# The second half of five loads on a second queue, and one cast on another engine

## The chip, the cores and the metric

The kernel runs on one core of a Trainium2 chip. The metric is the device time of one execution in microseconds (us), the median of several executions. The profile is that of one execution. Engines are named as the profile does: PE (TensorE), DVE (VectorE), ACT (ScalarE), POOL (GpSimd), SP (SyncE, which here only issues DMAs). A letter q behind an engine means its instruction queue: it issues or waits while the engine itself is idle.

## What is computed

A local and a pooled attention for 8 batches of 8 heads (576 positions, 64 elements), whose sum goes through a layer that mixes positions and channels:

```
q_d, k_d, v_d = means of 4 neighbouring positions of q, k, v        # 144 positions
out_up        = softmax(q_d k_d^T / 8) v_d, each position repeated 4 times
out_local     = softmax(q k^T / 8 where |i - j| < 4) v
x             = (out_up + out_local), heads side by side            # 8 x 576 x 512
theta         = x w_theta
u             = x + w_tok_r (x cos theta) + w_tok_i (x sin theta)
out           = u + max(u w_ch, 0)
```

Inputs and output are float32; the kernel works in bfloat16 with float32 sums.

## The kernel before

The kernel is a set of small generators, one for each step (load, cast, turns, scores and so on), each of which goes through all batches. A string, ORDER (line 66), says by one letter after the other which generator takes its next step; every instruction is pinned behind the one before it on its own engine (`pin`, line 758). So ORDER sets the order of the work on each engine, and nothing moves at run time: an engine whose next instruction waits lets nothing behind it pass. That holds for DMA issues too, which stand in the program order of the engine that issues them. ENGINES (line 86) names by one letter the engine of each copy or cast: v for VectorE, a for ScalarE, p for GpSimd.

**Loads** (`load`, line 220, letter L). A batch has 13 items in the order k0 k1 q0 q1 k2 k3 q2 q3 v0 v1 v2 v3 v4. A k or q item is one DMA of 128 partitions and 288 KB. A v item is two DMAs of 64 partitions and 128 KB each, one for each half of the partitions, since the two windows of positions that it holds overlap (line 225). Each item lands in one of 15 staging tiles, used in turn, and all loads are issued by SP. So batch 0 and the first two items of batch 1 find free tiles; a later item waits until the cast that read its tile is done.

The DMAs of the two hardware queues, SP's and ScalarE's, take eight completion semaphores in turn, and a DMA is issued when the earlier one with its semaphore has landed. Before, all are on SP: the first v DMA waits for k0, the next for k1, then q0, q1, k2 and so on.

**Casts** (`cast`, line 233, letter C) turn an item into bfloat16. In batch 0 the engines are: k0 and k1 VectorE; q0, q1 and k2 GpSimd; k3 ScalarE; q2 and q3 GpSimd; v0, v2, v4 ScalarE; v1, v3 GpSimd. The instruction is recorded at line 124.

**What follows for batch 0.** `turns` (line 291) transposes k and q on TensorE, 9 blocks for each of four pairs of items: k0 with k1, q0 with q1, k2 with k3, q2 with q3 (line 297). `turns_out` (line 300) copies the four results out of PSUM as kT and qT, for batch 0 all on ScalarE, where they stand right behind the cast of k3. `query_sums` (line 320; for batch 0 on VectorE, line 326) and `key_sums` (line 309, VectorE, line 314) add four neighbouring positions. `scores` and `scores_exp` (lines 465, 477) make the local scores and their exponentials, `masks` (line 485, VectorE) cuts them to the band. `pooled_scores` and `pooled_exp` (lines 379, 391, 398) do the pooled ones, `pooled_out` (lines 411, 417) multiplies with the pooled v, and `pooled_norm` divides on VectorE, beginning with the reciprocal at line 430. `outputs` (line 497) multiplies the masked scores with v.

On VectorE the order in this stretch is: constants, the sum of queries (326), two sums of keys (314), the second sum of queries, the first mask (485), and then the cast of batch 1's k0. On ScalarE it is: the table of functions, the cast of k3, four copies of kT and qT, the cast of v0, an exponential, the cast of v2, a pooled exponential (398), the cast of v4, and the next exponential (477).

The later steps (phases, mix, channels, lines 575 to 743) are large matmuls of 128 x 512 and make up most of TensorE's time.

Of the kernel before, what the change touches and what calls it, by code (L numbers as in the profile page):

```python
# [26 lines left out]
W = 64  # L27
# [18 lines left out]
def kernel(  # L46
# [11 lines left out]
    nc = tc.nc  # L58
# [5 lines left out]


    ORDER = (
        "kkLkLLCkkkLCLCCALCACALkCaLCAaakkkaeLSLLkkLCLsdCLSCCdeLmPLpLLCLCOLLoOCLLUluusPSpsALxCoiCxNLmCinnNaLnl"
        "nAllCClCdlLLAALLamaCaQeeTOOqdCooilitSLTtLLOPsLpoPTpmTliSCtHTCCUllstthuOHuoXmhXHlyOliyoOxxhVCHoiNhiCA"
        "CNlnvGnnCXnyCalAgOVQoVaTiqvVSvTCvtAstaCmCZVAHVVaOvovSVTLvsLTivetStXTlXytHVsHGlmVvHVvVhzLyLvhVvLLVgXe"
        "hVVLvvVvVJdjLyLLLLhJJCvCvLOvljOSJLmjoloCdsCCiCJilJjUOLjuuPPLpZCoClxziJmjxjpACXNaNyLLAnnCCCnOLXJanLyA"  # L70
# [14 lines left out]
    )  # L85
    ENGINES = dict(
        C=(
            "vvpppappapapavppvaaapvppppppppppppappppppapapappapvappappppppaapaaavvpapppapaapavvaapappaaapapaa"
            "vpaavpaa"
        ),  # L90
        a="aaaaaaaaaavaaaaavaaaaaaaaaaaaava",
# [2 lines left out]
        v="avaavaavvvvavvvava",  # L94
# [119 lines left out]
    def stage(key):  # L214
        t = staged[key] = rot("st", [P, S], FP32, 15)
        return t
# [3 lines left out]
    def load(b):  # L220
        for it in ITEMS:
            c = int(it[1])
            if it[0] == "v":
                t = stage((b, it))[:, 0:DM].rearrange("p (h d) -> p h d", d=D)
                for g in range(2):
                    lo = W0[2 * c + g]
                    nc.sync.dma_start(out=t[W * g:W * g + W], in_=v[b, :, lo:lo + W, :].rearrange("h p d -> p h d"))  # L227
            else:
                src = k if it[0] == "k" else q
                nc.sync.dma_start(out=stage((b, it)), in_=src[b, 2 * c:2 * c + 2].rearrange("h (p r) d -> (h p) (r d)", r=WR))  # L230
            yield
# [536 lines left out]
    def each(steps, n=B):  # L768
# [3 lines left out]
    sequences = {  # L772
        "k": constants(), "1": table(AF.Sin), "2": table(AF.Exp),
        "L": each(load), "C": each(cast), "l": weight_loads(), "V": weight_turns(), "v": weight_turns_out(),
        "A": each(turns), "a": each(turns_out), "d": each(key_sums), "e": each(query_sums),
        "U": each(pooled_v), "u": each(pooled_v_out), "x": each(pooled_v_last),
# [49 lines left out]
```

## Time and profile before

| what | us |
| --- | --- |
| three runs | 235.08, 233.96, 234.40 |
| their median | 234.4 |
| the profiled execution, its own time | 234.87 |
| its span, first to last instruction | 233.0 |
| busy: PE, DVE, ACT, POOL | 210.3, 196.1, 149.9, 83.1 |

The clock granted to TensorE was 0.991 of full speed on average. The hardware queue that SP feeds had packets in the 16 DMA engines for 82.2% of their span. Times in the profile count from the first instruction. A row of the timeline has the start, the length, the engine, the line, the operation, what it writes and reads, and in brackets how long the engine stood idle before it and what ended that. A line of the chain has a start, a length and what filled it.

### The profile page before, as it was taken

The page shows a single profiled execution, that of the slowest core. Times are in us where ns is not written, and L with a number is a line of the kernel's source. Part 1 is how long each engine was busy: PE and PEld are TensorE (multiplying, and loading weights), DVE is VectorE, ACT ScalarE, POOL GpSimd, SP SyncE. Part 2 cuts the span into 40 slices and gives each one's busy share as a digit, 9 for nine tenths or more (in the row PEclk, how much of TensorE's full clock was granted, in tenths as well). Part 3 has the DMA queues.
Part 4 walks back from the last instruction along what each step waited for, and adds up shares of the span by engine and source line. Part 5 has one row for each costly group of instructions (what it writes and reads, how often), then busy time and mean ns, then how long its engine had stood idle before and what let it go on. Part 6 is the DMA issues. An engine that isn't in the chain of part 4 may idle for free.

```text
span 233.0 us, 8062 instructions
## 1 busy us (share of the span) xinstructions
PE 210.3 (90%) x3309; PEld 134.1 (58%) x3344; DVE 196.1 (84%) x402; ACT 149.9 (64%) x220; POOL 83.1 (36%) x125
## 2 busy tenths in 40 slices
PE   0547959999999999999999999999999999999993
PEld 0435845877787547656666647565655674446441
DVE  3797998998988999998999888977999988395463
ACT  2376968999687976877899988399156366500000
POOL 1434987992555575534621503404032000000000
PEclk9999997999999999999999999999999999999999
DMA  6989999989997997996999999999135693858566
GB/s 205 284 188 344 201 182 334 258 123 176 341 225 148 264 303 146 254 275 149 260 277 264 183 197 347 256 244 217 19 70 138 93 171 126 124 165 214 125 187 251
DMA packets 87061, 48.52 MB, mean 208 GB/s; under 512 B 71920, under 2 KB 74352, under 8 KB 87024
## 3 DMA queue, kind: packets, MB, share of 16 engines
q1 hardware_dynamic: 84016, 44.84, 82.2%
q0 software_dynamic: 2496, 2.38, 7.2%
q10 hardware_dynamic: 512, 0.79, 1.0%
q8 instruction: 26, 0.43, 0.8%
q14 instruction: 11, 0.09, 0.2%
HBM read 34.11 MB, written 9.44 MB: 187 GB/s over the span
## 4 chain that ended last, share of the span: by engine, by line
PE 78%; DMA 8%; DVE 7%; SPq 4%; issue 2%; ACT 0%; DVEq 0%; ACTq 0%
PE space L668 30%; PE space L711 12%; PE space L575 11%; PE space L297 4%; PE space L537 3%; DMA st<-in_v_dram 3%; SPq L227 3%; PE space L497 3%; DMA st<-in_q_dram 2%; PE space L465 2%; DMA st<-in_k_dram 2%; PE space L627 2%; DVE tmp L517 2%; PE space L717 1%; PE space L411 1%
## 5 line engine op out<-in xcount | busy, mean ns | idle before, releaser
L668 PE MATMUL space<-WT,z 128*128 128x64 bf16 (+2 forms) x562 | 74.3, 284 | 1.1 <-issue 0.5
L668 PEld LDWEIGHTS <-z 128*128 128x128 bf16 x576 | 38.2, 98 | 28.7 <-issue 0.4
L575 PE MATMUL space<-wth,xT 128*128 128x512 bf16 x116 | 31.3, 388 | 0.7 <-issue 0.2
L711 PE MATMUL space<-wch,uT 128*128 128x512 bf16 (+1 forms) x125 | 31.2, 373 | 0.4
L684 DVE TENSOR_TENSOR uT<-space,xT 128x512 bf16<-128x512 f32 (+2 forms) x36 | 22.1, 620 | 8.0 <-PE space L668 7.8
L517 DVE TENSOR_TENSOR tmp<-space,rl 128x512 bf16<-128x512 f32 x40 | 26.7, 681 | 0.8 <-DVE rl L511 0.2
L560 DVE TENSOR_TENSOR xT<-space,xdT 128x464 bf16<-128x464 f32 (+3 forms) x42 | 24.5, 605 | 3.1 <-PE space L537 3.0
L477 ACT ACTIVATE pm<-space 128x1024 bf16<-128x1024 f32 (+1 forms) x24 | 21.1, 882 | 9.2 <-PE space L465 7.4
L582 ACT ACTIVATE cs<-space,pihc 128x512 bf16<-128x512 f32 x32 | 22.4, 700 | 5.4 <-PE space L575 2.9
L331 POOL TENSOR_TENSOR two<-qT 128x576 f32<-128x576 bf16 x14 | 17.2, 1229 | 20.8 <-ACT qT L124 20.6
L314 DVE TENSOR_REDUCE kd<-kT 128x290 bf16<-128x1160 bf16 x16 | 21.5, 1349 | 0.0
L124 POOL CAST q_tm<-st 128x576 bf16<-128x576 f32 x20 | 13.5, 677 | 18.8 <-DMA st<-in_q_dram 18.8
L725 DVE SCALAR_TENSOR_TENSOR osb<-space,ur 128x512 f32<-128x512 f32 x28 | 19.1, 682 | 1.1 <-PE space L711 1.0
L297 PE MATMUL space<-ident,k_tm 128*128 128x128 bf16 x144 | 12.5, 242 | 7.6 <-DVE k_tm L124 7.1
L583 ACT ACTIVATE cs<-space 128x512 bf16<-128x512 f32 x32 | 19.4, 607 | 0.0
L711 PEld LDWEIGHTS <-uT 128*128 128x128 bf16 x132 | 12.1, 98 | 11.8
L124 ACT COPY qT<-space 128x1152 bf16<-128x1152 bf16 x16 | 18.0, 1127 | 1.3 <-PE space L297 0.9
L124 POOL CAST v_w<-st 128x512 bf16<-128x512 f32 x19 | 12.6, 664 | 17.5 <-DMA st<-in_v_dram 13.4
L124 POOL CAST k_tm<-st 128x576 bf16<-128x576 f32 x16 | 11.2, 702 | 19.2 <-DMA st<-in_k_dram 19.0
L124 ACT COPY kT<-space 128x1152 bf16<-128x1152 bf16 x13 | 14.6, 1124 | 5.1 <-PE space L297 5.1
L575 PEld LDWEIGHTS <-xT 128*128 128x128 bf16 x128 | 11.5, 99 | 10.3 <-issue 0.5
L485 DVE TENSOR_TENSOR pm<-pm,band 128x1024 bf16<-128x1024 bf16 (+1 forms) x24 | 16.4, 693 | 1.0 <-ACT pm L477 1.0
(93 smaller groups left out, 369.7 us busy)
## 6 DMA issues: line engine op xcount, KB each, us to landing
st<-in_v_dram SPq DMA_DIRECT2D x80, 128.0 KB, 5.1
st<-in_k_dram SPq DMA_DIRECT2D x32, 288.0 KB, 5.3
st<-in_q_dram SPq DMA_DIRECT2D x32, 288.0 KB, 5.6
out_dram<-osb SPq DMA_DIRECT2D x28, 256.0 KB, 3.4
out_dram<-osb SPq DMA_DIRECT2D x6, 128.0 KB, 3.4
uT<-in_moe_w_tok_r_dram POOLq DMA_DIRECT2D x6, 108.0 KB, 6.6
uT<-in_moe_w_tok_i_dram POOLq DMA_DIRECT2D x6, 108.0 KB, 5.5
wth<-in_moe_w_theta_dram POOLq DMA_DIRECT2D x4, 128.0 KB, 6.5
```

The source lines that it names most:

```text
L124: copies[next(engines[step])](**operands)
L297: nc.tensor.transpose(out=ps[:, P * r:P * r + P], in_=(k_tm if what == "k" else q_tm)[:, i, r, :, :], identity=ident)
L314: nc.vector.tensor_reduce(out=kd[:, hs, :, 0:PG].rearrange("p e g m -> p (e g) m"), axis=AX.X, op=ALU.add, in_=kT[:, hs, :].rearrange("p e ...
L477: nc.scalar.activation(out=pm.rearrange("p e c j w -> p e (c j w)"), in_=held.pop(("S", b, u))[:, :, 0:4 * W * n], func=AF.Exp, scale=SCL)
L517: nc.vector.tensor_tensor(out=tmp.rearrange("p g (j d) -> p g j d", d=D), in0=held.pop(("loc", b, c))[:, :, :, 0:D], in1=rls.pop((b, c)).u ...
L560: nc.vector.tensor_tensor(out=xTs[b][i][:, :, lo:lo + n].rearrange("p e (m j) -> p e m j", j=4), in0=ps[:, :, at:at + n].rearrange("p e (m ...
L575: nc.tensor.matmul(out=th, lhsT=xT[:, dc, P * c:P * c + P], rhs=wth[:, dc, :], start=(dc == 0), stop=(dc == 3))
L582: nc.scalar.activation(out=cs[:, 0, :], in_=th, func=AF.Sin, bias=pihc, scale=1.0)
L583: nc.scalar.activation(out=cs[:, 1, :], in_=th, func=AF.Sin, bias=0.0, scale=1.0)
L668: nc.tensor.matmul(out=ps[:, n * i:n * i + n], lhsT=z[:, j, P * d:P * d + P], rhs=WT[:, j, lo:lo + n], start=(j == 0), stop=(j == 8))
L684: nc.vector.tensor_tensor(out=uT[:, dc, lo:lo + m], in0=ps[:, 0:m], in1=xT[:, dc, lo:lo + m], op=ALU.add)
L711: nc.tensor.matmul(out=ps, lhsT=uT[:, dc, P * c:P * c + P], rhs=wch[:, dc, cols], start=(dc == 0), stop=(dc == 3))
```

## The change

Three edits go together.

1. In batch 0, the second half of each v load (g = 1) is issued by ScalarE's queue instead of SP's.
2. The third cast, that of q0 of batch 0, goes from GpSimd to ScalarE.
3. In ORDER, the loads from k3 to v4 of batch 0 come right after the third cast. Only the letters L move; without them the old and the new string are the same. On SP, which does nothing else there, this changes no order. It sets where ScalarE's five issues stand: behind its cast of q0 and ahead of its cast of k3.

```
     ORDER = (
-        "kkLkLLCkkkLCLCCALCACALkCaLCAaakkkaeLSLLkkLCLsdCLSCCdeLmPLpLLCLCOLLoOCLLUluusPSpsALxCoiCxNLmCinnNaLnl"
+        "kkLkLLCkkkLCLCLLLLLLLLCACACAkCaCAaakkkaeSkkCsdCLSCCdeLmPLpLLCLCOLLoOCLLUluusPSpsALxCoiCxNLmCinnNaLnl"
...
     ENGINES = dict(
         C=(
-            "vvpppappapapavppvaaapvppppppppppppappppppapapappapvappappppppaapaaavvpapppapaapavvaapappaaapapaa"
+            "vvappappapapavppvaaapvppppppppppppappppppapapappapvappappppppaapaaavvpapppapaapavvaapappaaapapaa"
...
                 for g in range(2):
                     lo = W0[2 * c + g]
-                    nc.sync.dma_start(out=t[W * g:W * g + W], in_=v[b, :, lo:lo + W, :].rearrange("h p d -> p h d"))
+                    queue = nc.scalar if b == 0 and g else nc.sync
+                    queue.dma_start(out=t[W * g:W * g + W], in_=v[b, :, lo:lo + W, :].rearrange("h p d -> p h d"))
```

The program that is built from it has on ScalarE, in this order: the table of functions, the cast of q0, the five issues, the cast of k3, and then what stood behind it before. The eight semaphores are still taken in turn, so that the waits of the v issues become:

| half | issued by | waits for the landing of |
| --- | --- | --- |
| v0, second | ScalarE | k0 |
| v0, first | SP | k1 |
| v1, second | ScalarE | q0 |
| v1, first | SP | q1 |
| v2, second | ScalarE | k2 |
| v2, first | SP | k3 |
| v3, second | ScalarE | q2 |
| v3, first | SP | q3 |
| v4, second | ScalarE | v0, second half |
| v4, first | SP | v0, first half |

The next load on SP, k0 of batch 1, waits for the landing of v1's second half, and k1 of batch 1 for v1's first half. The order of the instructions on TensorE and VectorE is the same as before; GpSimd lacks its first cast.

## The prediction

> **What bounds the kernel now.** The page comes first: the span, and the engines' shares of the chain that ended last.
>
> ```profile
> span 233.0 us, 8062 instructions
> PE 78%; DMA 8%; DVE 7%; SPq 4%; issue 2%; ACT 0%; DVEq 0%; ACTq 0%
> ```
>
> TensorE has 78% of the chain, so a change in the first 20 us counts only by how much later or earlier the long busy stretch begins. The busy time by stretches says where that stretch starts (columns: length, then busy us and instructions of PE, PEld, DVE, ACT, POOL, granted clock, DMA share, GB/s).
>
> ```profile
> 12.00:16.00 4.00, 2.62 (x81) 2.06 (x81) 3.82 (x8) 3.44 (x5) 0.95 (x2) 1.00 0.78 174
> 20.00:34.00 14.00, 10.37 (x216) 8.62 (x212) 13.82 (x25) 10.45 (x14) 12.04 (x19) 1.00 1.22 235
> 34.00:57.00 23.00, 22.20 (x439) 15.62 (x441) 20.97 (x47) 21.50 (x35) 18.09 (x29) 0.93 1.02 222
> 57.00:230.00 173.00, 169.99 (x2513) 104.08 (x2541) 148.88 (x280) 108.15 (x163) 47.70 (x65) 1.00 0.89 202
> ```
>
> From 20 to 34 us VectorE is busy 13.82 of 14.00; from 34 us TensorE is busy 22.20 of 23.00, then 169.99 of 173.00. Nothing after 20 us has room to give back a late start, and an early start would be kept too. So the question is how VectorE's work moves between 9 and 25 us. I read that stretch engine by engine in the timeline (start, length, engine, line, operation; in brackets the idle time before it and what ended it). ScalarE:
>
> ```profile
> 9.40 0.67 ACT L124 CAST k_tm<-st 128x576 bf16<-128x576 f32 x1 [7.38 <-DMA st<-in_k_dram]
> 9.98 1.11 ACT L124 COPY kT<-space 128x1152 bf16<-128x1152 bf16 x1
> 10.99 1.12 ACT L124 COPY qT<-space 128x1152 bf16<-128x1152 bf16 x1
> 18.37 0.89 ACT L398 ACTIVATE pd<-space 128x864 bf16<-128x864 f32 x1 [1.51 <-PE space L379]
> 19.66 1.03 ACT L477 ACTIVATE pm<-space 128x1024 bf16<-128x1024 f32 x1
> ```
>
> VectorE:
>
> ```profile
> 12.14 1.35 DVE L326 TENSOR_REDUCE qdT<-qT 128x288 bf16<-128x1152 bf16 x1 [1.23 <-ACT qT L124]
> 17.85 0.68 DVE L485 TENSOR_TENSOR pm<-pm,band 128x1024 bf16<-128x1024 bf16 x1
> 20.11 0.75 DVE L124 CAST k_tm<-st 128x576 bf16<-128x576 f32 x1 [1.58 <-DMA st<-in_k_dram]
> 25.11 0.19 DVE L430 RECIPROCAL rd<-space 72x8 f32<-72x8 f32 x1
> ```
>
> TensorE:
>
> ```profile
> 17.98 0.34 PE L379 MATMUL space<-qdT,kd 64*64 64x144 bf16 x4 [2.02 <-DVE qdT L326]
> 20.74 0.33 PE L379 MATMUL space<-qdT,kd 64*64 64x144 bf16 x4 [0.63 <-ACT pm L477]
> 21.59 0.62 PE L465 MATMUL space<-qT,kT 64*64 64x64 bf16 x16 [0.16 <-DVE vd L124]
> 22.18 1.12 PE L297 MATMUL space<-ident,k_tm 128*128 128x128 bf16 x9
> 23.59 0.87 PE L417 MATMUL space<-vd,pd 128*72 128x260 bf16 x2
> ```
>
> The chain of this stretch: the cast of k3 on ScalarE at 9.40, two copies behind it in program order, then VectorE's sum at 12.14, which had stood idle 1.23 for the second copy. From there VectorE runs without a gap to the end of the mask, 17.85 + 0.68 = 18.53, and then waits 1.58 for the first k load of batch 1. So **ScalarE's cast of k3 is on the path**, and behind it lies 1.58 of slack that a late load makes.
>
> **The change part by part.** *The third cast* (q0) leaves GpSimd for ScalarE.
>
> ```profile
> 6.12 0.66 POOL L124 CAST q_tm<-st 128x576 bf16<-128x576 f32 x1 [4.81 <-DMA st<-in_q_dram]
> 8.50 0.67 POOL L124 CAST k_tm<-st 128x576 bf16<-128x576 f32 x1
> 10.49 0.67 POOL L124 CAST q_tm<-st 128x576 bf16<-128x576 f32 x1 [1.32 <-DMA st<-in_q_dram]
> 11.67 0.67 POOL L124 CAST q_tm<-st 128x576 bf16<-128x576 f32 x1 [0.50 <-DMA st<-in_q_dram]
> ```
>
> q0 lands at 6.12. ScalarE takes 0.67 for that shape (its 9.40 row) and idled 7.38 up to 9.40, so the cast runs from 6.12 to 6.79 at no cost; GpSimd loses 0.66 where it idled. If that idle time were gone it would cost 0.67.
>
> *The five issues on ScalarE* follow this cast in its program order, and k3's cast stands behind all five. Each load waits for the semaphore that an earlier load used: v0's second half for k0, v1's for q0, v2's for k2, v3's for q2, and **v4's for the landing of v0's second half**. That such a wait holds a queue can be seen on SP, in the chain in order of time, where the fourth issue of v starts as q1 lands; the last two rows are a v issue that nothing held and the issue of batch 1's k0.
>
> ```profile
> 2.12 5.62 DMA st<-in_q_dram
> 7.75 0.94 SPq L227
> 12.66 0.63 SPq L227
> 14.69 0.62 SPq L230
> ```
>
> With 0.63 + 0.04 an issue: the first two at 6.8 and 7.5; the third needs k2, cast at 8.50 and so landed by then, and ends about 9.2; the fourth needs q2, landed at 10.49, and ends at 11.1; the fifth needs v0's second half. Its landing time is unknown. The nearest rows are the issues of v before, all ten and then the first alone (it sits in the 4.78 row):
>
> ```profile
> L227 SPq DMA_DIRECT2D st<-in_v_dram x10: 632/720/2522, 4.8 to 14.0; - x10
> DMA to landing us min/median/max: 3.3/5.0/7.3
> 4.78 0.81 SPq L227 DMA_DIRECT2D st<-in_v_dram  x1
> DMA to landing us min/median/max: 7.3/7.3/7.3
> ```
>
> Issued at 6.8 it lands between 6.8 + 3.3 = 10.1 and 6.8 + 7.3 = 14.1. I take 12.0, where its other half landed before (4.78 + 7.3): both share the engines with the same k and q loads. The median, 5.0, gives 11.8, nearly the same. So the fifth issue ends at 12.0 + 0.65, and k3's cast starts at 12.65, **D = 3.25 late**. At the early end the fourth issue decides, k3 starts at 11.8, D = 2.4; at the late end 14.75, D = 5.35.
>
> The trace shows the 16 DMA engines at a share of 0.78 between 12 and 16 us and of 1.02 and more in the busy stretches: there is a little room while v loads go out one at a time, and no more. [...]
>
> *What D does.* Everything from the copy at 9.98 to the mask is in program order behind k3's cast. VectorE's sum starts at 12.14 + 3.25, the mask ends at 18.53 + 3.25 = 21.78. The cast of batch 1's k0 no longer waits and starts at about 21.75 instead of 20.11: 1.65 late on this branch. The other branch has no such slack: the products at 17.98 wait for VectorE's sums, the exponential at 18.37 for them, the one at 19.66 stands behind it, and the products at 20.74 waited for that one. They come at 24.0. Behind them TensorE runs nearly closed up to the end of L417, 23.59 + 0.87 = 24.46, less the 0.16 that L465 need not wait any more: 24.46 + 3.25 - 0.16 = 27.55. VectorE's reciprocal at 25.11 reads that result, so it comes 27.55 - 25.11 = 2.4 late, the later of the two branches. From there VectorE was full.
>
> *The five issues taken from SP.* Nothing but loads stands behind them. Before, batch 1's k0 was issued at 14.69; now it waits for v1's second half, issued at 7.5, by the median landing at 12.5: about 2 earlier. That is worth at most VectorE's 1.58, already counted as slack here. GpSimd's queue carries no load of this stretch. v0 to v4 are cast behind the copies and are there in time.
>
> **Sum:** +3.25 (k3's cast) - 0.16 - 0.65 (24.46 to 25.11) = **+2.4 us**. The profiled execution took 234.87 (span 233.0), which gives 237.3; the median of the runs shown is 234.4, which gives **236.8**. With D = 2.4 the net is 1.6 (236.0), with D = 5.35 it is 4.5 (238.9).
>
> **Rivals.** *It is not slower.* The mechanism: ScalarE is free again when k3 lands, k0 of batch 1 lands earlier, and VectorE's wait of 1.58 goes with no other in its place. The gain ends at the other branch, whose result at 24.46 - 0.16 lies 0.8 ahead of 25.11: 234.4 - 0.8 = 233.6, and 232.7 if the cold stretch below goes too. For it speak the wait itself and the DMA share of 0.78. It decides if k3's cast starts less than 0.8 after 9.40; against it, the fourth issue waits for q2, which landed at 10.49. q2 would have to land some 1.6 sooner, in the same queue behind the same loads.
>
> *The clock.* The granted clock fell once before the last microseconds:
>
> ```profile
> 33.50:34.00 0.50, 0.40 (x8) 0.28 (x5) 0.50 (x3) 0.50 (x2) 0.27 (x1) 1.00 1.03 130
> 34.50:35.00 0.50, 0.50 (x20) 0.24 (x10) 0.50 (x2) 0.24 (x2) 0.41 (x2) 0.50 0.94 178
> 37.00:37.50 0.50, 0.50 (x8) 0.05 (x3) 0.46 (x1) 0.49 (x2) 0.50 (x2) 0.50 0.84 283
> 37.50:38.00 0.50, 0.49 (x20) 0.35 (x21) 0.50 (x2) 0.50 (x2) 0.50 (x2) 0.90 1.07 415
> 32.12 0.32 PE L497 MATMUL space<-v_w,pm 64*64 64x65 bf16 x16 [1.60 <-DVE tmp L517]
> 37.04 0.62 DVE L560 TENSOR_TENSOR xT<-space,xdT 128x448 bf16<-128x448 f32 x1 [0.92 <-PE space L537]
> ```
>
> It is 0.50 from about 34 to 37.5, some 3.4 us, behind a stretch in which TensorE idled 1.60, and VectorE waited 0.92 for TensorE in it. Shifted work can miss this: with D = 2.4 the time is 236.0 - 0.9 = 235.1, no change by the bound below. Or it is met once more: 236.8 + 0.9 = 237.7. [...]
>
> *The loads slow each other.* KB and median time to landing of the loads:
>
> ```profile
> st<-in_v_dram SPq DMA_DIRECT2D x80, 128.0 KB, 5.1
> st<-in_q_dram SPq DMA_DIRECT2D x32, 288.0 KB, 5.6
> ```
>
> q2 and q3 landed 11.67 - 10.49 = 1.18 apart, so two v halves that go ahead of them hold them up by about 2 x 128 / 288 x 1.18 = 1.0 (an estimate from these rows). Then v0's second half lands at 13.0 too, D is 4.25 and the time 237.8. If SP finishes no sooner (its last v half waits for v0's first, at 12.0), nothing changes: k0 of batch 1 is not what is late.
>
> **How the numbers follow.** About 0.5% is what a measurement of this kernel can tell from no change: 233.2 to 235.6 is the same. The forecast, ScalarE held by its loads, 235.6 to 239: 0.72 (the slowed loads are 0.15 and the second cold stretch 0.08 of it). More than 239: 0.03. Within 0.5%: D of 2.4 with the cold stretch gone, 235.1, at 0.12, and the free ScalarE, 233.6, at 0.06; together 0.18. Faster, the free ScalarE with the cold stretch gone, 232.7: 0.07. The range 235.0 to 239.0 leaves out 0.07 + 0.06 + 0.03 and a part of the 235.1.
>
> **What would show it.** Right: ScalarE's first idle time is ended by q0's landing at about 6.1, k3's cast starts between 11.8 and 13.5, VectorE's first sum of queries at about 15.4, the 1.58 wait for batch 1's k0 is gone, and the reciprocal L430 comes near 27.5. Wrong: k3's cast before 10.3 (the issues did not hold ScalarE), or a late start that the stretch 20 to 57 us gives back, which would show as idle time of VectorE there that is in the trace of before and that the busy columns hide.

## The result and the profile after

| | before | after |
| --- | --- | --- |
| median of six runs each, us | 234.3 | 237.18 |
| the six, lowest to highest | 233.62 to 235.29 | 235.96 to 238.62 |
| the profiled execution / its span | 234.87 / 233.0 | 237.11 / 235.3 |
| k3's cast on ScalarE starts | 9.40 | 13.12 |
| VectorE's first sum of queries starts | 12.14 | 15.86 |
| the first reciprocal (L430, after: L431) starts | 25.11 | 27.97 |

The changed kernel is **slower by 1.2%**: the ratio is 1.0121, with a 95% interval from 1.0072 to 1.017. From line 227 on, the line numbers of the changed kernel are one higher than before. Medians and ratios here and below are of executions that were not disturbed.

The page of the changed kernel: the span, the shares of the chain that ended last, and the hardware queue of ScalarE (packets, MB, share of the 16 DMA engines).

```profile
span 235.3 us, 8097 instructions
q10 hardware_dynamic: 3152, 1.44, 3.0%
PE 78%; DMA 9%; DVE 6%; ACT 3%; issue 2%; SPq 1%; DVEq 0%; ACTq 0%
```

The second queue had 512 packets and 0.79 MB before; the rest is the five halves. ScalarE, at 0% of the chain before, now has 3% of it. The timeline of ScalarE in the changed kernel shows how:

```profile
5.71 0.67 ACT L124 CAST q_tm<-st 128x576 bf16<-128x576 f32 x1 [3.69 <-DMA st<-in_q_dram]
5.72 7.36 ACTq L228 DMA_DIRECT2D st<-in_v_dram  x5
13.12 0.67 ACT L124 CAST k_tm<-st 128x576 bf16<-128x576 f32 x1 [6.74 <-DMA st<-in_v_dram]
13.70 1.11 ACT L124 COPY kT<-space 128x1152 bf16<-128x1152 bf16 x1
14.71 1.12 ACT L124 COPY qT<-space 128x1152 bf16<-128x1152 bf16 x1
22.08 0.89 ACT L399 ACTIVATE pd<-space 128x864 bf16<-128x864 f32 x1 [2.05 <-PE space L380]
23.38 1.03 ACT L478 ACTIVATE pm<-space 128x1024 bf16<-128x1024 f32 x1
```

The second row is the one to learn from: ACTq is the queue, and the five issues reach from 5.72 to 13.08, although the five, of 0.60 to 0.72 us each, make 3.25. The rest is waiting inside the queue: the third issue began at 8.12, where k2 had landed at 8.10, the fourth at 9.85 (q2 at 9.82), the fifth at 12.47. The third row names what ended the wait: the cast of k3 came after an idle time of 6.74, ended by the landing of a v load, a tensor that this cast does not read. The copies follow without a gap. VectorE and TensorE of the changed kernel, from the timeline:

```profile
15.86 1.35 DVE L327 TENSOR_REDUCE qdT<-qT 128x288 bf16<-128x1152 bf16 x1 [5.30 <-ACT qT L124]
21.57 0.68 DVE L486 TENSOR_TENSOR pm<-pm,band 128x1024 bf16<-128x1024 bf16 x1
21.70 0.34 PE L380 MATMUL space<-qdT,kd 64*64 64x144 bf16 x4 [2.07 <-DVE qdT L327]
22.16 0.75 DVE L124 CAST k_tm<-st 128x576 bf16<-128x576 f32 x1
23.78 0.69 DVE L124 CAST vd<-space 128x512 bf16<-128x512 f32 x1 [0.76 <-PE space L346]
24.46 0.33 PE L380 MATMUL space<-qdT,kd 64*64 64x144 bf16 x4 [0.63 <-ACT pm L478]
27.97 0.20 DVE L431 RECIPROCAL rd<-space 72x8 f32<-72x8 f32 x1 [0.77 <-PE space L418]
```

VectorE waited 1.23 for the second copy before, now 5.30. The cast of batch 1's k0 (22.16) has no bracket any more: its wait of 1.58 is gone. Two brackets are new: the cast of vd waited 0.76 for TensorE's L346, and the reciprocal 0.77 for its L418. So VectorE is no longer what is late at this place; the branch through TensorE and the exponentials is.

The stretches of the changed kernel (columns as in the prediction):

```profile
12.00:16.00 4.00, 2.06 (x22) 1.90 (x26) 0.14 (x1) 2.88 (x4) 0.61 (x1) 1.00 1.37 200
20.00:34.00 14.00, 9.09 (x208) 7.48 (x209) 12.41 (x20) 10.94 (x15) 9.95 (x15) 1.00 1.07 222
34.00:57.00 23.00, 21.28 (x450) 14.95 (x450) 21.88 (x48) 19.60 (x29) 20.01 (x32) 0.93 0.86 193
57.00:230.00 173.00, 172.95 (x2570) 105.08 (x2569) 149.57 (x283) 110.57 (x169) 47.94 (x66) 1.00 0.88 200
```

From 12 to 16 us VectorE worked 0.14 of 4.00 instead of 3.82: that is where the time goes. A mark for how much of it lasts is the first large matmul of the mix over positions (the fourth number is its start). Before, and then after:

```profile
L668 PE MATMUL space<-WT,z x30: 286/286/296, 56.7 to 60.9; 128*128 128x288 bf16 x30
```

```profile
L669 PE MATMUL space<-WT,z x15: 286/286/296, 59.3 to 61.0; 128*128 128x288 bf16 x15
```

It starts 2.6 later, and the span is 2.3 longer. The reciprocal was 2.86 late. So the loss is made in the first 28 us, and all that follows gives back some 0.5 of it.

### The profile page after: what moved, and what is told of

The parts are those of the page before. It is cut to its first block, busy times and chain, and to the rows that moved or that the text cites. A ratio compares the mean times of both kernels' runs of the same rounds, so it can differ in the third digit from the quotient of the medians.

```text
span 235.3 us, 8097 instructions
## 1 busy us (share of the span) xinstructions
PE 210.7 (90%) x3344; PEld 133.2 (57%) x3344; DVE 195.4 (83%) x402; ACT 149.8 (64%) x221; POOL 82.7 (35%) x124
## 4 chain that ended last, share of the span: by engine, by line
PE 78%; DMA 9%; DVE 6%; ACT 3%; issue 2%; SPq 1%; DVEq 0%; ACTq 0%
PE space L669 31%; PE space L712 12%; PE space L576 10%; DMA st<-in_v_dram 5%; PE space L298 5%; DMA st<-in_q_dram 3%; PE space L538 3%; PE space L466 2%; PE space L498 2%; PE space L628 2%; PE space L412 2%; DVE tmp L518 2%; PE space L718 1%; PE space L594 1%; PE space L418 1%
## 5 line engine op out<-in xcount | busy, mean ns | idle before, releaser
L669 PE MATMUL space<-WT,z 128*128 128x512 bf16 (+2 forms) x576 | 75.9, 286 | 0.0
L576 PE MATMUL space<-wth,xT 128*128 128x512 bf16 x128 | 32.1, 381 | 0.0
L298 PE MATMUL space<-ident,k_tm 128*128 128x128 bf16 x144 | 12.0, 236 | 12.1 <-DVE k_tm L124 7.1
L361 POOL TENSOR_TENSOR vd<-last,own 128x256 bf16<-128x256 bf16 x16 | 10.7, 676 | 23.6 <-ACT last L124 17.4
L124 POOL CAST q_tm<-st 128x576 bf16<-128x576 f32 x19 | 12.7, 676 | 16.9 <-DMA st<-in_q_dram 16.9
L124 POOL CAST v_w<-st 128x512 bf16<-128x512 f32 x19 | 11.9, 639 | 18.0 <-DMA st<-in_v_dram 12.4
L298 PEld LDWEIGHTS <-k_tm 128*128 128x128 bf16 x144 | 10.0, 106 | 13.2 <-DVE k_tm L124 7.1
```

The source lines that it names most:

```text
L124: copies[next(engines[step])](**operands)
L298: nc.tensor.transpose(out=ps[:, P * r:P * r + P], in_=(k_tm if what == "k" else q_tm)[:, i, r, :, :], identity=ident)
L576: nc.tensor.matmul(out=th, lhsT=xT[:, dc, P * c:P * c + P], rhs=wth[:, dc, :], start=(dc == 0), stop=(dc == 3))
L669: nc.tensor.matmul(out=ps[:, n * i:n * i + n], lhsT=z[:, j, P * d:P * d + P], rhs=WT[:, j, lo:lo + n], start=(j == 0), stop=(j == 8))
```

## The experiments

**The theory:** ScalarE runs in order, the five issues wait for the landings of other loads, and k3's cast, the copies and VectorE's sum stand behind them. **The rivals:** the second queue costs time by itself, because the v halves take bandwidth from k and q or delay SP's loads; or the cast of q0 or the moved loads cost it. A table of all runs comes first; ratios are to the kernel before, run on the same chip in the same set of runs (its medians in the three sets of the experiments were 234.3, 234.6 and 234.3). A ratio with its interval is as recorded; it is not the quotient of the two medians, which for the hold alone would be 1.0144. Starts are those of the profiled execution, in us.

| kernel | median | ratio (95%) | k3's cast | first sum | reciprocal | mix | span |
| --- | --- | --- | --- | --- | --- | --- | --- |
| before | 234.3 | | 9.40 | 12.14 | 25.11 | 56.7 | 233.0 |
| after | 237.18 | 1.0121 (1.0072 to 1.017) | 13.12 | 15.86 | 27.97 | 59.3 | 235.3 |
| hold alone, one queue | 237.7 | 1.0105 (1.0064 to 1.0146) | 12.95 | 15.69 | 27.80 | 59.3 | 235.7 |
| third cast alone | 235.16 | 1.0022 (0.9987 to 1.0057) | 8.54 | 11.29 | 24.53 | 57.3 | 233.3 |
| four issues | 235.03 | 1.0019 (0.999 to 1.0048) | 9.93 | 12.67 | 24.78 | 56.8 | 233.0 |
| three issues | 234.32 | 0.9986 (0.9948 to 1.0023) | 8.08 | 10.83 | 23.21 | 54.9 | 232.5 |
| three issues, again | 235.66 | 1.0055 (1.001 to 1.0101) | 7.59 | 10.33 | 23.24 | 55.3 | 231.9 |
| five issues, other semaphores | 236.87 | 1.0081 (1.0046 to 1.0116) | 10.39 | 13.13 | 25.24 | 56.3 | 232.9 |
| the same, a second execution | 237.85 | | 11.36 | 14.10 | 26.21 | 58.0 | 236.1 |
| four issues, other semaphores | 235.61 | 1.0027 (0.9993 to 1.006) | 8.53 | 11.27 | 24.57 | 57.6 | 234.2 |
| after, two copies on VectorE | 235.1 | 1.0016 (0.999 to 1.0042) | 12.97 | 13.26 | 25.36 | 56.7 | 233.5 |
| before, two copies on VectorE | 235.79 | 1.0072 (1.0041 to 1.0103) | 9.10 | 13.51 | 25.61 | 57.3 | 234.0 |
| three issues, k3 on GpSimd | 234.68 | 1.0033 (1.0 to 1.0066) | GpSimd | 10.66 | 23.79 | 56.2 | 233.2 |

**The hold alone, without a second queue.** All loads go on SP and the third cast on GpSimd, as before. What holds ScalarE is another wait of the same length: the cast of v0 is put ahead of k3's. (A tiny exponential at the start keeps the table load, of 1.28 us, at 0.74, where it is before too; the casts keep their engines.)

```
-        "kkLkLLCkkkLCLCLLLLLLLLCACACAkCa...
+        "kk2LkLLCkkkLCLCLLLLLLLLCACACCAkCa...
...
-            "vvappappapapavppv...
+            "vvpppaapppapavppv...
...
-                    queue = nc.scalar if b == 0 and g else nc.sync
+                    queue = nc.sync
...
-        for it in ITEMS:
+        for it in (ITEMS if b else ITEMS[:5] + ["v0"] + ITEMS[5:8] + ITEMS[9:]):
```

> All loads on SP and the third cast on GpSimd as before; the cast of v0 is put ahead of k3's cast on ScalarE, so that k3's cast is held by the landing of v0 without any second queue (a tiny activation at the start loads the function table). v0 landed at 12.5 before; k3's cast then starts at about 13.1, D = 3.7, as in the changed kernel. Theory: +2.4 to +3.2, 236.7 to 237.5. Rival (the two queues get in each other's way in the DMA engines): no second queue, so no change, 234.3.

Its timeline:

```profile
12.43 0.62 ACT L124 CAST v_w<-st 128x512 bf16<-128x512 f32 x1 [10.19 <-DMA st<-in_v_dram]
12.95 0.67 ACT L124 CAST k_tm<-st 128x576 bf16<-128x576 f32 x1
27.80 0.20 DVE L431 RECIPROCAL rd<-space 72x8 f32<-72x8 f32 x1 [0.77 <-PE space L418]
```

k3's cast starts at 12.95 (after: 13.12), the reciprocal at 27.80 with the same wait of 0.77 for TensorE (after: 27.97), and the ratio is 1.0105 against 1.0121 (the median, 237.7, is 0.2 above the range expected). No DMA of this kernel is on another queue than before. The hold by itself is enough for the whole loss. That ScalarE's issues *are* such a hold is what the next runs show.

**The cast alone, and fewer issues.** The changed kernel with all its loads on SP (ORDER and the third cast stay as changed), and with four or three of the five halves on ScalarE; the line is given for each, in this order:

```
-                    queue = nc.scalar if b == 0 and g else nc.sync
+                    queue = nc.sync
+                    queue = nc.scalar if b == 0 and g and c < 4 else nc.sync
+                    queue = nc.scalar if b == 0 and g and c < 3 else nc.sync
```

> The third cast on ScalarE and the order of the changed kernel, but all loads on SP. Theory (the change costs its time because k3's cast stands behind ScalarE's issues and their waits): no difference from before, 234.3, k3's cast at about 9.4. Rival (moving q0's cast is part of the cost): up to 0.7 slower, 235.0.

> The second halves of v0 to v3 on ScalarE, that of v4 back on SP. The wait for v0's second half goes; the wait of v3's for q2, landed at 9.8, stays. Theory: k3's cast at about 10.5, D = 1.1, net 0.2 to 0.6 slower: 234.5 to 234.9. Rival (contention, in proportion to the halves moved): four fifths of 2.9, 236.6.

> The second halves of v0 to v2 on ScalarE, those of v3 and v4 on SP. The last of ScalarE's three issues waits for k2, landed at about 8, and ends at about 8.7, before k3 lands. Theory: k3's cast is not held, D at most 0; 233.5 to 234.5 (a gain up to 0.8). Rival (the second queue itself costs, by the number of halves): three fifths of 2.9, 236.2.

The cast alone has no cost clear of noise: 1.0022, and the interval holds 1. So edits 2 and 3 are not the loss. A part of it, up to 0.6%, the interval does not exclude, and the median of 235.16 is near the rival's 235.0. Four issues came 0.1 above their range, three within it. The timeline with four issues, and then with three:

```profile
5.75 4.13 ACTq L228 DMA_DIRECT2D st<-in_v_dram  x4
9.93 0.67 ACT L124 CAST k_tm<-st 128x576 bf16<-128x576 f32 x1 [3.50 <-DMA st<-in_q_dram]
```

```profile
5.72 2.33 ACTq L228 DMA_DIRECT2D st<-in_v_dram  x3
8.08 0.67 ACT L124 CAST k_tm<-st 128x576 bf16<-128x576 f32 x1 [1.70 <-DMA st<-in_k_dram]
```

The brackets of the k3 rows name, one after another, the waits that the table of semaphores in front lists: with four issues the last landing is a q load's (q2), with five a v load's (v0's second half). With three it is a k load's, and the trace has two of them close together: k2 landed at 7.20, the third issue waited for it and ended at 8.04, and k3 itself landed at 7.93. So nearly nothing of the hold is left there. The **fifth** issue alone moves k3's cast from 9.93 to 13.12 and the ratio from 1.0019 to 1.0121. With four, D is 0.53, and the time is that of before.

**Five issues with other semaphores.** All five halves stay on ScalarE, but the semaphores are dealt out so that they wait for k0, k1, q0, q1 and k2, all landed by the time of the issue; SP's first halves come behind them. One function for a half, called for the five second halves ahead of the first ones:

```
+                def half(c, g):
...
+                if b == 0 and c == 0:
+                    for n in range(5):
+                        stage((b, f"v{n}"))
+                        half(n, 1)
```

> All five second halves on ScalarE as in the changed kernel, but the semaphores are dealt first to ScalarE's five and then to SP's five, so that ScalarE's wait for k0, k1, q0, q1 and k2 instead of k0, q0, k2, q2 and v0's second half. Theory: issues at 5.7 to 9.2, k3's cast at about 9.3, D about 0; 233.5 to 234.5. Rival (contention of the queues, or the 0.6 to 0.7 us that each issue takes on ScalarE): still near 237.

This was **a miss**: 236.87, not 233.5 to 234.5. The first profile is of the fastest of its executions, 234.70, in which k3's cast still started 0.99 late (10.39). So a second execution was profiled.

> A second profile of e5, whose first profiled execution was its fastest, at a granted clock of 1.0. Theory: in an execution near its median the fifth issue is held longer, k3's cast at 11 to 12, and the clock falls to half once. Rival: k3's cast at 10.4 again and the time lost after 25 us.

That execution took 237.85, longer than all but one of the twelve before it. Its issues (columns: minimum, median and maximum in ns, first and last start), and the timeline around them:

```profile
L228 ACTq DMA_DIRECT2D st<-in_v_dram x5: 643/657/1870, 6.6 to 9.5; - x5
```

```profile
8.17 0.72 POOL L124 CAST k_tm<-st 128x576 bf16<-128x576 f32 x1
11.36 0.67 ACT L124 CAST k_tm<-st 128x576 bf16<-128x576 f32 x1 [4.06 <-DMA st<-in_v_dram]
26.21 0.20 DVE L447 RECIPROCAL rd<-space 72x8 f32<-72x8 f32 x1 [0.77 <-PE space L434]
144.88 1.15 POOL L348 TENSOR_TENSOR two<-qT 128x576 f32<-128x576 bf16 x1
144.91 1.66 DVE L502 TENSOR_TENSOR pm<-pm,band 128x1024 bf16<-128x1024 bf16 x1 [0.75 <-ACT pm L494]
```

The last issue waits for k2, which GpSimd casts at 8.17, so it has landed by then. Yet the issue, begun at 9.5, takes 1.87 instead of 0.66, and k3's cast starts only at 11.36. So this issue held its engine for 1.87 although the load that it waits for had landed. (The bracket names a v load here too, though no issue of this kernel on ScalarE waits for one: the bracket tells what came last before the end of a wait, and that need not be its cause.) Without the late semaphore k3's cast is 0.99 and 1.96 late, with it 3.72; the difference, 1.8 to 2.7, is about what the wait for v0's second half adds. SP shows the same in the kernel before: of its ten v issues one took 2.52, the longest in the row that the prediction shows, where the fourth, at 7.75, had taken 0.94. It is the next, the fifth, which waits for k2, landed at 8.45:

```profile
8.74 2.52 SPq L227 DMA_DIRECT2D st<-in_v_dram  x1
```

The 2.52 on SP, the 1.87 here and 1.29 in the first profile of this kernel have in common that four v halves were outstanding on the queue. That this number is the cause was not tried, and it is not enough by itself: on SP, before, the next two issues, at 11.30 and 11.98, took 0.64 and 0.63, with five and six halves outstanding (the first landed at about 12.0). The rest of the miss lies elsewhere: here the reciprocal is 1.1 late and the span 3.1 longer, so that both the theory and the rival of the second expectation came true in part. 0.97 of the difference is the mask at 144.91, to which the last section comes back. Some 0.7 of the other 1.0 arose between the masks that start at 115.94 and 137.43 (21.49 apart, 20.83 before); what made it is open. **So the hold of k3's cast does not account for the whole time of this kernel**, and a cost of five issues on the second queue with these semaphores is not excluded.

**Four issues with other semaphores** (waits for k0, k1, q0, q1): the same edit with four halves on ScalarE, the fifth on SP.

> Four second halves on ScalarE with the semaphores dealt as in e5: they wait for k0, k1, q0 and q1. In e5 the fifth issue on ScalarE took 1.29 with four v halves outstanding, as the fifth v issue on SP takes 2.3 to 2.5 in e1 and before; here there is no fifth. Theory (what costs is how long k3's cast is held): issues end at about 8.9, k3's cast at 9.0 to 9.3, D at most 0: 233.5 to 234.6. Rival (dealing ScalarE's semaphores first delays something on SP that counts, which would also explain e5): as e5, about 236.5.

Its timeline:

```profile
8.53 0.67 ACT L124 CAST k_tm<-st 128x576 bf16<-128x576 f32 x1 [2.15 <-DMA st<-in_k_dram]
19.58 0.75 DVE L124 CAST k_tm<-st 128x576 bf16<-128x576 f32 x1 [1.92 <-DMA st<-in_k_dram]
```

With early semaphores and four issues the hold is gone: k3's cast waits for k3 itself. 1.0027, with 1 in the interval. The time was a miss all the same: 235.61 lies between its range, 233.5 to 234.6, and the rival's 236.5, and only the ratio speaks against the rival. Nothing is gained by the early start: VectorE now waits 1.92 for batch 1's k0, and the span is 1.2 longer than before although the reciprocal is 0.5 earlier.

**The copies taken out from behind the hold.** If the way from the hold to the loss is ScalarE's two copies, it is cut by giving these to VectorE, with all five issues and the waits left as changed. The control is the kernel before with the same move.

```
-        a="aaaaaaaaaavaaaaavaaaaaaaaaaaaava",
+        a="vvaaaaaaaavaaaaavaaaaaaaaaaaaava",
```

> The changed kernel with the first two copies out of PSUM (kT and qT of the first pair) on VectorE, so that they no longer stand behind k3's cast. ScalarE is held as before, k3's cast at about 13. VectorE does the copies from about 8.3, then its constants (2.9) and its first sum at about 13.5 instead of 15.9. Theory: D for VectorE falls from 3.7 to about 1.4, net about 0.5: 234.9. Rival (contention of the queues, not the hold): still near 237.

> The kernel before with the first two copies out of PSUM (kT and qT of the first pairs) on VectorE instead of ScalarE; all loads stay on SP. Held ScalarE: in the kernel with five issues on ScalarE the same move of the copies took the hold off the path (235.1). If nothing else of the second queue costs time, this kernel, which has no second queue, is as long: VectorE's own constants then stand ahead of its first sum of queries, which starts near 13.5, and the reciprocal comes near 25.5; 234.9 to 235.4. Rival (the second queue has a cost of its own, which the move of the copies left in): this kernel is 0.8 or more faster than 235.1.

The changed kernel with this move, in the timeline:

```profile
12.97 0.67 ACT L124 CAST k_tm<-st 128x576 bf16<-128x576 f32 x1 [6.90 <-DMA st<-in_v_dram]
13.26 1.34 DVE L327 TENSOR_REDUCE qdT<-qT 128x288 bf16<-128x1152 bf16 x1
```

ScalarE is held exactly as long (k3's cast at 12.97), but VectorE's sum starts at 13.26 instead of 15.86, and the ratio falls from 1.0121 to 1.0016. The control, which has no second queue, is not faster than this: 1.0072. So the second queue shows no cost of its own here. The control missed its range by 0.4 and is slower than the kernel with the second queue; why is open.

**Looking for a version that wins.** Three issues had the earliest start. It was run with k3's cast on GpSimd as well, so that the copies stand right behind the third issue, and once more as it was.

```
-            "vvappappapapavppv...
+            "vvapppppapapavppv...
```

> Three second halves on ScalarE's queue (c < 3), as in the kernel with three issues, and k3's cast on GpSimd, so that ScalarE's two copies stand right behind its third issue. Held ScalarE: the copies start near 8.1 and 9.1, VectorE's first sum near 10.3 (10.83 with k3's cast on ScalarE); the reciprocal comes near 22.8 (23.21). If an early start were kept to the end: 232.2. If the overlaps of VectorE with GpSimd and the loads take it back, as they took back 1.4 of the 1.9 of the kernel with three issues: 234.0 to 234.6. Slower than 235 if GpSimd's next cast (q2) is late by k3's 0.67.

> The kernel with three second halves on ScalarE once more. In its first profile VectorE's reciprocal came at 23.21 instead of 25.11, and 1.4 of these 1.9 were lost between 100 and 205 us, most of it at 143 us where a mask on VectorE took 1.55 instead of 0.68 beside work of GpSimd. If that give-back is fixed by the order of the program: 234.3, a ratio of 0.998 to 1.000. If it was chance: 233.0, a ratio of 0.994.

Neither beats the kernel before: 1.0033, and 1.0055 where the first run of three issues gave 0.9986. With k3's cast on GpSimd the reciprocal came at 23.79, 1.0 later than expected, and the time, 234.68, at the upper end of the range for a head start that is taken back. The second run fits neither of its expectations (0.998 to 1.000, or 0.994), so of three issues no more can be said than that they do not win. The reciprocal is 1.9 earlier in both profiles with three issues, and the span only 0.5 and 1.1 shorter. A part of the way back can be seen. One mask on VectorE in the first of them, beside what GpSimd did at that time:

```profile
141.39 1.15 POOL L332 TENSOR_TENSOR two<-qT 128x576 f32<-128x576 bf16 x1
141.53 1.55 DVE L486 TENSOR_TENSOR pm<-pm,band 128x1024 bf16<-128x1024 bf16 x1 [0.74 <-ACT pm L478]
```

And the same mask in the kernel before:

```profile
140.30 1.15 POOL L331 TENSOR_TENSOR two<-qT 128x576 f32<-128x576 bf16 x1
141.52 0.67 POOL L332 TENSOR_TENSOR qdT<-two 128x288 bf16<-128x288 f32 x1
142.96 0.69 DVE L485 TENSOR_TENSOR pm<-pm,band 128x1024 bf16<-128x1024 bf16 x1 [0.74 <-ACT pm L477]
```

0.69 where GpSimd is done, 1.55 where an instruction of GpSimd had begun just before it: 0.86 of the head start is lost at this one instruction. In the second run of three issues this mask missed GpSimd, and there the profiled execution was the shorter one (a span of 231.9); its median, 235.66, says that this was not the rule.

## Why the prediction was right

The forecast was 236.8 (+2.4 on the median); measured were 237.18 (+2.9), on the profiled executions 237.11 - 234.87 = 2.24, where 2.4 was worked out.

*The hold.* Right in place and cause: the first idle time of ScalarE was ended by q0 at 5.71 (said: about 6.1), that before the cast of k3 by the landing of a v load, and with four issues by q2's. **Its size was 0.47 too small**: D is 13.12 - 9.40 = 3.72, not 3.25. The third, fourth and fifth issues waited where they were said to wait, and the term that was mis-sized is the landing of v0's second half, taken at 12.0 by its other half before. The trace has the fifth issue from 12.47 to 13.08, so the half had landed by 12.47. Two errors partly cancel in the 12.0: the first issue was put behind the cast of q0, at 6.8, and began beside it, at 5.72; and the half took some 6.7 to land, where 5.2 was left for it. The range for k3's cast, 11.8 to 13.5, held it.

*What D does.* From k3's cast to VectorE's sum all things move together: 15.86 - 12.14 = 3.72, the same D. The sum came later than the 15.4 said only by what D had been set too small. VectorE's wait of 1.58 is gone, TensorE's branch is the later one, and the reciprocal moved by 2.86 = D - 0.86, where D - 0.81 was predicted. Batch 1's k0 was issued at 13.47, 1.2 earlier and not 2, and VectorE did not wait for it. In VectorE's branch two things were not foreseen, and they nearly cancel: it was held 0.76 for TensorE's L346, and its second mask took 0.69 instead of 1.59. With 1.59 VectorE would have come to the reciprocal at about 28.1 instead of 27.97 (27.97 - 0.77 + 0.90), so the time rests little on this.

*Luck.* That 2.24 came so near to 2.4 is in part luck. D was 0.47 too small, and the late start was to be kept whole behind the reciprocal; of the 2.86 there, 2.6 were left at the mix and 2.3 at the end.

*The sentence that an early start would be kept was wrong.* A late start was: 2.86 and 2.69 at the reciprocal became 2.3 and 2.7 (most of the one, all of the other) in the spans of the changed kernel and of the hold alone. An early one was not: 1.9 became 0.5 and 1.1 with three issues, and with four, or with k3 on GpSimd, nothing. The working took a busy VectorE for one that has no room and nothing to lose. But its busy time is not fixed. Of the 13.82 us that it was busy from 20 to 34, 1.59 are one mask, which took 0.69 in the changed kernel. The second mask of the kernel before, and then of the changed kernel, with GpSimd's work beside it, in the timeline:

```profile
22.79 0.67 POOL L124 CAST q_tm<-st 128x576 bf16<-128x576 f32 x1
22.99 1.59 DVE L485 TENSOR_TENSOR pm<-pm,band 128x1024 bf16<-128x1024 bf16 x1
23.42 0.61 POOL L360 TENSOR_TENSOR vd<-last,own 128x256 bf16<-128x256 bf16 x1
```

```profile
25.92 0.69 DVE L486 TENSOR_TENSOR pm<-pm,band 128x1024 bf16<-128x1024 bf16 x1
25.95 1.12 POOL L361 TENSOR_TENSOR vd<-last,own 128x256 bf16<-128x256 bf16 x1
```

The first mask of the kernel before, at 17.85, took 0.68 with GpSimd idle. Before, GpSimd's cast had begun ahead of the second mask, and the mask took 1.59 while GpSimd kept its times. In the changed kernel the mask began 0.03 ahead of the same instruction of GpSimd, took 0.69, and that instruction was the longer one, 1.12 instead of 0.61. So the shift of the start changed here which of the two took longer. And an early engine meets loads that do not come earlier, as the 1.92 above shows.

*The rivals.* "ScalarE is free again when k3 lands" fell, since q2 was cast at 9.88 and landed a little before, at 9.82. Its condition, k3's cast less than 0.8 after 9.40, was made by experiment with four issues (0.53), and the time was then the same as before (1.0019) and not the 233.6 of that rival: the gain it hoped for from the lost wait of 1.58 does not exist. "The loads slow each other" fell too; GpSimd's casts of q2 and of batch 1's k1 in the changed kernel, from the timeline, the first at 10.49 before (k1 landed some 1.1 earlier than before, too):

```profile
9.88 0.67 POOL L124 CAST q_tm<-st 128x576 bf16<-128x576 f32 x1 [1.06 <-DMA st<-in_q_dram]
19.74 0.67 POOL L124 CAST k_tm<-st 128x576 bf16<-128x576 f32 x1 [2.39 <-DMA st<-in_k_dram]
```

q2 came 0.6 earlier, not 1.0 later. Some 0.4 of that q0 already had, 5.71 against 6.12, before the second queue issued anything; from q0's cast to q2's it is 4.17, where it was 4.37. Before, too, v halves were under way (SP began the fourth at 7.75), so what is compared is two queues with one. The trace does not bear out this rival's estimate, that the v halves make q2 late. And no kernel with a second queue was faster than before by more than the noise: the lowest ratio is 0.9986 (0.9948 to 1.0023).

*The clock.* It fell to 0.50 once before the last microseconds in both profiled executions; in the changed kernel from about 35 to 38.4, as long as before (3.4) and 0.8 later (windows of 0.5 us, clock third from the end):

```profile
34.50:35.00 0.50, 0.00 (x1) 0.00 (x1) 0.50 (x2) 0.00 (x0) 0.50 (x2) 1.00 1.15 297
35.00:35.50 0.50, 0.43 (x16) 0.29 (x15) 0.50 (x2) 0.00 (x0) 0.50 (x2) 0.52 1.13 314
```

So it does not enter the difference of these two profiles. What makes it fall was not shown. It may be a part of the scatter: one of the six executions after had an average granted clock of 1.0, and it was the fastest, 235.96, still above all six of before.

## What to carry to other kernels

A DMA issue on ScalarE was here an instruction in that engine's program: while it waited for the landing of an older load (the fifth ended at 13.08, and the cast began at 13.12), or took longer without such a wait (1.87, the cast at 11.36), the cast behind it waited too. Before moving issues off an idle queue, list for each of them whose landing it waits for and what stands behind the last one. Here four issues had no cost clear of noise (1.0019, with 1 in the interval), and the fifth, which waited for a load just issued, brought the cost to 1.2%. An early semaphore alone did not make five issues free here: with it the ratio was still 1.0081. And price a late start and an early start apart: of the first 2.3 of 2.86 us were kept here, of the second 0.5 and 1.1 of 1.9.

## What was not expected of the hardware

- An issue that stood behind a cast on ScalarE did not wait for the cast's end: in the changed kernel the cast of q0 starts at 5.71, with a length of 0.67, and the first issue at 5.72.
- Three issues took longer although the load that they wait for had landed: 1.29 and 1.87 us for the fifth v half on ScalarE's queue, 2.52 on SP's, against some 0.6 to 0.7 for the others on ScalarE. What held them was not shown.
- A mask on VectorE (128 x 1024) took 0.68 or 0.69 us in the rows in which GpSimd did nothing, and 1.59, 1.55 and 1.66 in three rows in which GpSimd had begun an instruction 0.03 to 0.20 before it (22.99 before, 141.53 with three issues, 144.91 with five issues and other semaphores). Where the mask began 0.03 ahead of GpSimd's TENSOR_TENSOR (25.92 after) it took 0.69, and the TENSOR_TENSOR 1.12 instead of 0.61. Not every row is like these: at 33.79 before, a mask took 0.64 with a cast of GpSimd begun 0.05 ahead of it, and there the cast was the longer one, 1.17 where others of its shape took 0.62. Which of the two took longer changed with the start, and so a shift of the start was not simply carried to the end.
